# Attention and feed-forward in one kernel: constants built in three parts, two score pairs moved into the steps, products of ones, GEMM pieces and PSUM banks dealt out anew

## The chip, the cores and the metric

The kernel runs on one core of a Trainium2 chip. The metric is the time of one execution in device microseconds (us); lower is better. TensorE (PE, with its weight loads PEld), VectorE (DVE), ScalarE (ACT), GpSimd (POOL) and SyncE (SP, which here only issues DMAs) each run their own instructions in program order and wait for one another by semaphores.

## The reference, cut to what matters

```python
scores = scale * q @ k^T                                 # (4, 12, 448, 448): batch, head, row, column
scores = einsum('bhij,hg->bgij', scores, w_pre)          # premix: mixes the 12 heads
attn = exp(scores - max); attn = attn / (sum + 1e-9)
attn = einsum('bhij,hg->bgij', attn, w_post)             # postmix
x = (attn @ v), heads side by side                       # (1792, 768)
h = x @ w_in; r = maximum(h, 0); g = s * r * r + b       # w_in 768 x 2048
out = g @ w_out                                          # w_out 2048 x 768
```

All inputs are float32. The kernel keeps float32 accuracy by splitting an operand into a rounded high part and a low part, and adding three products (low by high, high by low, high by high).

## The kernel before, in words

**Chunks and blocks.** The rows of the scores are cut into 16 chunks (4 per batch, of 110 or 118 rows), and each chunk into 11 or 12 blocks of up to 10 rows, 180 blocks (`NB`) in all. A block holds 10 rows of all 12 heads on 120 partitions, so that the mixing of heads is a product with a 120x120 matrix (`wpre_hi`, `wpre_lo`: `w_pre` repeated along a diagonal of blocks; `wpost` likewise).

**Scores of a chunk.** `qk_part` (line 469) does a pair of heads in three products each; six pairs make a chunk. The result goes from PSUM into the tile `S` of the chunk with the scale 1/8. In most pairs both heads lie in the one two-bank PSUM tile `sc`, and one ACT instruction copies both (line 495). In chunks 0 and 1 the odd pairs are `apart`: each head takes a bank of its own, by `bank()`, and DVE copies them, one after the other (line 493). `relayout` (line 547) is a DMA on SP that gathers a block from all 12 heads of `S` into `blk`; it needs the whole chunk. `split` (line 555) on POOL makes the high and low part `hl` (lines 559, 560).

**Steps.** After a prologue the kernel runs one step `s` per block (line 805). In program order step `s` holds `relayout(s+5)`, `split(s+2)`, `normalize(s-1)` (DVE reciprocal, line 591; ACT scaling into `eh`, line 593), `evacuate(s-3)` (line 631 on DVE; line 629 on ACT for the last chunk), `premix(s)` (line 565: three products into a PSUM tile `pm`, DVE maximum on line 574, ACT exponential on line 579 in place, its sum on line 583), `remainder(s-1)` (DVE, line 600), `postmix(s-2)` (12 products on line 615), and what a plan puts there: loads of q, k, v, the transposes `prep_q` and `prep_k`, score pairs (`qk_pair`) of later chunks, pairs of attention times v (`av_pair`, line 513), pieces of the first GEMM (`head_piece`: three products on line 247). The plan is a list made at build time from costs and due times (lines 642 to 731). From step 12 on, each step also does one instruction of the conversion of a weight (`conversion`, lines 145 to 180).

**Prologue** (lines 756 to 803). Loads; then the pairs of chunk 0, among them the transposes of k by `prep_k`, whose low part is a DVE instruction (line 232) that is put off until the next `low_parts()`. `keep_busy(n)` issues n products of a tile of ones, 128x512, into a PSUM tile that nobody reads. Then `build_consts` (line 340): 14 DVE instructions that make `wpre_hi`, `wpre_lo`, the scale `xscale` and `wpost`. Then five relayouts, two splits, `prep_q` of chunk 1, and the six pairs of chunk 1.

**Tail of the attention and start of the GEMMs.** The first GEMM (`gemm1_part`, line 242) makes `ph` tiles of 18 products for batch b and a block f of 128 columns of `w_in`. Three of them (b = 0, f = 0 to 2) are done in 18 pieces ahead: 12 by the plan in steps 167 to 179, 6 after the last step. After the steps come conversions (`convert_to`), the last chunk's six `av_pair`s and the 6 pieces, one more conversion (line 842), the splitting of batch 1's x (`split_x`, lines 212 to 225: ACT line 223 for the high part, DVE line 232 for the low part), and the loop over the `ph` tiles; ACT's `relu2` (lines 252 to 267) takes each. Their banks come from `bank()` (line 237), which deals out six banks in the fixed order of `banks` = pm, po, pm, po, xp, px by a count `turn["bank"]`; the prologue's 22 calls have moved that count on. The pieces' tiles are `sc` (two banks) and, for f = 2, `px`. Two GEMM rounds follow, the second GEMM on line 300.

Of the kernel before, what the change touches and what calls it, by code (L numbers as in the profile page):

```python
# [21 lines left out]
def talking_heads_attention__then__act_relu2_kernel(  # L22
# [316 lines left out]

    def build_consts(mask, rep, wall):  # L340
        kron = smp.tile([BP, BI, H], F32, tag="kron", name="kron", bufs=1)
# [9 lines left out]

        mx = smp.tile([P, 4], F32, tag="mx", name="mx", bufs=1)
        nc.vector.tensor_reduce(out=mx[:, 0:1], in_=wall, axis=AX.X, op=ALU.max)
# [5 lines left out]
        nc.vector.tensor_scalar(mu[:, 3:4], mu[:, 2:3], 0x7F800000, None, op0=ALU.bitwise_xor)  # L359
        nc.vector.tensor_scalar_mul(xscale, mx[:, 2:3], 2.0 ** -29)  # L360
        kron2 = smp.tile([BP, H, BI], F32, tag="kron2", name="kron2", bufs=1)
        nc.vector.tensor_tensor(
# [106 lines left out]
    def qk_part(ci, p, m):  # L469
# [4 lines left out]
        qt, kt = q_t[ci], k_t[b, p]  # L474
        apart = ci < 2 and p % 2 == 1
        if m == 0 and apart:
# [14 lines left out]
        if apart:  # L491
            for e in range(2):
                nc.vector.tensor_scalar_mul(s_t[ci][:n, 2 * p + e, :], sc[e][:n, :S], SCALE)
        else:
            nc.scalar.activation(  # L495
                s_t[ci][:n, 2 * p:2 * p + 2, :], x_t["two"][:n, :, :S], AF.Copy, scale=SCALE
            )
# [67 lines left out]
    def premix(t):  # L565
        n = blocks[t][2] * H
        hl = hl_t.pop(t)

        tag = "px" if t % 3 == 2 else "pm"
        pm = ps.tile([P, 512], F32, tag=tag, name=f"pm_{t}", bufs=banks.count(tag))  # L570
        for m, (w, x) in enumerate(((wpre_lo, 0), (wpre_hi, 1), (wpre_hi, 0))):
            nc.tensor.matmul(pm[:n, :S], w[:n, :n], hl[:n, x, :], start=(m == 0), stop=(m == 2))  # L572
        st = smp.tile([BP, 4], F32, tag="st", name=f"st_{t}")
        nc.vector.tensor_reduce(  # L574
            out=st[:n, 0:1], in_=pm[:n, :S], axis=AX.X, op=ALU.max, negate=True
        )

        e = pm[:, :S]
        nc.scalar.activation(e[:n], e[:n], AF.Exp, bias=st[:n, 0:1], accum_out=pm[:n, S:S + 1])  # L579
        e_t[t] = (e, st)  # L580

        total = pm[:, S:S + 1]
        nc.scalar.activation(
            st[:n, 2:3], total[:n], AF.Copy, scale=2.0 ** -15, bias=1e-9 * 2.0 ** -15
        )
# [113 lines left out]
    for i in range(NHEAD * NKC):  # L699
        if i < NHEAD * NKC - LATE:  # L700
            when = w0 + i * (NB + 3 - w0) / (NHEAD * NKC - LATE)
            fill.append((when, w0 + i // 2, NB + 2, 0.567, 1, head_piece, ()))
        else:
# [71 lines left out]
    for p in range(NP):  # L775
        low_parts()
        if p + 2 < NP:
            prep_k(0, p + 2)
        if p == 1:
            low_parts()  # L780
            prep_q(0, 1)
            low_parts()
        for m in range(3):
            qk_part(0, p, m)
        if p < 3:
            keep_busy(1)
    banks.append("px")
    build_consts(*loaded_consts)
    for t in range(LD):
        relayout(t)  # L790
    for t in range(LS):
        split(t)

    for half in range(2):
        prep_q(1, half)
    low_parts()
    for p in range(NP):
        for m in range(3):
            qk_part(1, p, m)
    while plan[0][0] < 0:  # L800
        x = plan.pop(0)
# [3 lines left out]
    for s in range(NB + 3):  # L805
# [17 lines left out]
        if s < NB:  # L823
            premix(s)
        low_parts()
        if 0 <= s - 1 < NB:
            remainder(s - 1)
# [13 lines left out]
    run_plan(NB + 100, False)  # L841
    convert_to(NU_EARLY + 3)
    att.close()
# [6 lines left out]
    for kc in range(NKC):  # L850
        split_x(0, 1, kc)
        low_parts()
    for r in range(NR):
        u0 = 2 * r * NU
# [90 lines left out]
```

## Time and profile before

| | |
|---|---|
| time, median of 3 runs | 968.75 us (968.42 to 970.42) |
| the profiled execution: its own time | 969.14 us |
| its span, first to last instruction | 967.4 us |
| mean granted TensorE clock | 0.993 |
| busy: PE, DVE, ACT, POOL | 928.9, 640.2, 595.8, 397.1 us |
| steps 0 to 179 | premixes from 30.1 to 486 us of the span |
| first GEMM's first full tile, after the pieces | 500.95 us |

All times in the text are us from the start of the span. An engine that is idle costs time only where the work that ends last waits for it. A row of the timeline that holds several instructions of one line is marked x and their number; its duration is that of the lot.

### The profile page before, as it was taken

How to read it: one execution, taken by the hardware profiler on the slowest of the kernel's cores; microseconds unless marked ns; L12 is line 12 of the kernel's file. 1: busy time of each engine (PE TensorE's matmuls, PEld its weight loads, DVE VectorE, ACT ScalarE, POOL GpSimd, SP SyncE). 2: the span in 40 equal slices, each digit the busy share in tenths (PEclk: the TensorE clock that was granted, in tenths of full speed). 3: DMA queues.
4: the chain of work that ended last, by engine and by line, in shares of the span. 5: the costliest groups of instructions: out<-in, count | busy, mean ns of one | idle time of the engine just before them, and what ended most of it. 6: DMA issues, size and time to landing. Idle time of an engine off the chain costs nothing.

```text
span 967.4 us, 19864 instructions
## 1 busy us (share of the span) xinstructions
PE 928.9 (96%) x7515; PEld 786.4 (81%) x7515; DVE 640.2 (66%) x1314; ACT 595.8 (62%) x1315; POOL 397.1 (41%) x469
## 2 busy tenths in 40 slices
PE   6889999999999999999989999999999999999998
PEld 3656767777777777777779999999998999999998
DVE  4789999888878888788678217746716811849311
ACT  3587777777888888888777878422216787711000
POOL 3766667666676667666613323100001332310000
PEclk8899999999999999999999999999999999999999
DMA  4665645654455544645422302234431410237431
GB/s 103 165 152 143 173 115 147 174 135 136 122 138 145 134 129 116 154 123 160 121 70 90 123 23 84 82 115 139 147 139 42 154 59 1 69 112 215 144 99 50
DMA packets 124252, 114.63 MB, mean 118 GB/s; under 512 B 61656, under 2 KB 120044, under 8 KB 124156
## 3 DMA queue, kind: packets, MB, share of 16 engines
q1 hardware_dynamic: 114630, 101.69, 38.1%
q10 hardware_dynamic: 9366, 11.59, 3.4%
q8 instruction: 59, 0.97, 0.4%
q0 software_dynamic: 160, 0.09, 0.1%
q14 instruction: 37, 0.30, 0.1%
HBM read 58.28 MB, written 16.52 MB: 77 GB/s over the span
## 4 chain that ended last, share of the span: by engine, by line
PE 65%; ACT 14%; DVE 14%; DMA 4%; issue 2%; POOL 1%; SPq 0%; ACTq 0%; DVEq 0%; POOLq 0%
PE po L300 24%; PE ph L247 16%; PE po L615 6%; PE pm L572 5%; PE xp L513 5%; PE sc L485 5%; ACT S L495 4%; ACT pm L579 3%; DVE eh L600 3%; ACT eh L593 3%; DVE A L631 2%; DVE st L574 2%; DMA nq<-in_q_dram 1%; PE trk L438 1%; DMA blk<-S 1%
## 5 line engine op out<-in xcount | busy, mean ns | idle before, releaser
L300 PE MATMUL po<-w,g 128*128 128x384 f32 x1344 | 234.6, 336 | 2.6 <-ACT h L255 2.6
L300 PEld LDWEIGHTS po<-w,g 128*128 128x128 f32 x1344 | 233.7, 188 | 3.3 <-ACT h L255 3.2
L560 POOL TENSOR_TENSOR hl<-blk,hl 120x448 fp32r<-120x448 f32 x180 | 205.8, 1143 | 15.0
L265 POOL TENSOR_TENSOR g<-h,g 128x448 fp32r<-128x448 f32 x64 | 77.7, 1214 | 291.5 <-ACT g L264 278.2
L615 PEld LDWEIGHTS <-eh 120*128 120x128 f16 (+1 forms) x2160 | 115.8, 98 | 65.8 <-DVE eh L600 42.5
L247 PE MATMUL ph<-x,w 128*128 128x448 f32 x810 | 166.1, 364 | 0.0
L559 POOL TENSOR_SCALAR hl<-blk 120x448 fp32r<-120x448 f32 x180 | 104.5, 581 | 141.7 <-PE pm L572 124.5
L247 PEld LDWEIGHTS ph<-x,w 128*128 128x128 f32 x810 | 151.9, 188 | 12.1
L615 PE MATMUL po<-wpost,eh 120*128 120x120 f16 (+1 forms) x2160 | 145.6, 218 | 16.6 <-DVE eh L600 14.9
L579 ACT ACTIVATE pm<-pm,st 120x448 f32<-120x448 f32 x180 | 109.8, 610 | 56.4 <-DVE st L574 55.8
L600 DVE SCALAR_TENSOR_TENSOR eh<-pm,st,eh 120x448 f16<-120x448 f32 x180 | 122.1, 678 | 18.0 <-ACT eh L593 14.7
L593 ACT ACTIVATE eh<-pm,st 120x448 f16<-120x448 f32 x180 | 114.2, 634 | 18.5 <-DVE st L591 16.1
L574 DVE TENSOR_REDUCE st<-pm 120x1 f32<-120x448 f32 x180 | 111.0, 617 | 22.0 <-PE pm L572 20.5
L631 DVE COPY A<-po 128x480 f32<-128x480 f32 x168 | 106.8, 636 | 0.1
L572 PE MATMUL pm<-hl,wpre_hi 120*120 120x448 f32 x360 | 102.9, 367 | 0.7 <-POOL hl L560 0.7
L495 ACT ACTIVATE S<-sc 110x896 f32<-110x896 f32 (+1 forms) x90 | 82.5, 917 | 22.0 <-PE sc L485 17.5
L513 PE MATMUL xp<-A,v 128*64 128x110 f32 (+1 forms) x1536 | 93.7, 265 | 0.6 <-ACT A L629 0.6
L153 ACT ACTIVATE mk<-raw 128x384 f32<-128x384 f32 x64 | 35.4, 553 | 91.7 <-DMA raw<-in_moe_w_out_dram 35.0
L485 PE MATMUL sc<-Tk,Tq 64*110 64x448 f32 (+1 forms) x576 | 84.4, 400 | 5.6 <-DVE Tq L232 3.6
L513 PEld LDWEIGHTS xp<-A,v 128*64 128x64 f32 x1536 | 74.2, 136 | 10.2 <-ACT A L629 1.1
L572 PE MATMUL pm<-hl,wpre_lo 120*120 120x448 f32 x180 | 82.1, 456 | 0.0
L232 DVE TENSOR_TENSOR x<-xraw,x 128x448 fp32r<-128x448 f32 x36 | 24.1, 695 | 76.9 <-ACT x L223 76.9
(74 smaller groups left out, 999.8 us busy)
## 6 DMA issues: line engine op xcount, KB each, us to landing
blk<-S SPq DMA_DIRECT2D x172, 210.0 KB
raw<-in_moe_w_in_dram SPq DMA_DIRECT2D x32, 384.0 KB
raw<-in_moe_w_out_dram SPq DMA_DIRECT2D x32, 384.0 KB
xraw<-xd SPq DMA_DIRECT2D x48, 224.0 KB
part<-ob ACTq DMA_DIRECT2D x28, 192.0 KB
acc<-part SPq DMA_DIRECT2D x28, 192.0 KB
out_dram<-acc ACTq DMA_DIRECT2D x28, 192.0 KB
v<-in_v_dram SPq DMA_DIRECT2D x24, 192.0 KB
```

What stands on the lines that cost most here:

```text
L247: nc.tensor.matmul(ph[:, :S], w[:, i, c0:c0 + P], x[:, y, :], start=(kc == 0 and m == 0), stop=(kc == NKC - 1 and m == 2),)
L300: nc.tensor.matmul(po[:, :NO], g[:, x, c0:c0 + P], w[:, y, :], start=(f == 0 and m == 0), stop=(f == NF - 1 and m == 2),)
L485: nc.tensor.matmul(sc[e][:n, :S], qt[r0:r0 + D, p, x, :n], kt[r0:r0 + D, y, :], start=(m == 0), stop=(m == 2),)
L513: nc.tensor.matmul(xp[e * D:(e + 1) * D, p % 4, :n], vt[:, e, c, :], a[:, c, 2 * p + e, :n], start=(c == 0), stop=(c == NC - 1),)
L560: nc.gpsimd.tensor_tensor(out=hl[:n, 1, :], in0=blk[:n], in1=hl[:n, 0, :].bitcast(F32), op=ALU.subtract)
L572: nc.tensor.matmul(pm[:n, :S], w[:n, :n], hl[:n, x, :], start=(m == 0), stop=(m == 2))
L574: nc.vector.tensor_reduce(out=st[:n, 0:1], in_=pm[:n, :S], axis=AX.X, op=ALU.max, negate=True)
L579: nc.scalar.activation(e[:n], e[:n], AF.Exp, bias=st[:n, 0:1], accum_out=pm[:n, S:S + 1])
L593: nc.scalar.activation(eh[:n, 0, :], e[:n], AF.Copy, scale=st[:n, 3:4])
L600: nc.vector.scalar_tensor_tensor(out=eh[:n, 1, :], in0=e[:n], scalar=st[:n, 3:4], in1=eh[:n, 0, :], op0=ALU.mult, op1=ALU.subtract,)
L615: nc.tensor.matmul(po[:, c * BP:(c + 1) * BP], eh[:n, x, j0:j0 + P], wpost[:n, y].rearrange("p g i -> p (g i)"), start=(m == 0), stop=(m = ...
L631: nc.vector.tensor_copy(dst, src)
```

## The change

`build_consts` becomes three functions: `build_pre` (3 DVE instructions: the premix matrix) runs after `prep_q` of chunk 1 and ahead of its pairs, `build_scale` (7) within step 0, `build_post` (4) within step 1, each behind that step's premix. Chunk 1's pairs 4 and 5 move from the prologue into steps 0 and 1, right behind these; pair 5 now uses the two-bank tile. The copies of the remaining odd pairs are shared: ACT copies the first head, DVE the second. In the prologue the low part of k's last transpose is put ahead of pair 3, and one product of ones is dropped. `premix` gets products of ones into its own `pm` tile, ahead of its three: two in steps 0 to 9, one in steps 10 to 13, 24 in all. Of the 12 pieces that the plan spread, 8 are now spread over steps 167 to 175, and 4 kept for steps 179, 180 (two) and 181; two pairs of attention times v move with them. The count of the banks is set to 0 ahead of the GEMMs, and the conversion of line 842 is put behind `split_x` of batch 1.

```diff
--- before.py
+++ after.py
@@ -337,7 +337,9 @@
         nc.gpsimd.dma_start(sb[:, 1:2], moe_b.rearrange("(o n) -> o n", o=1).to_broadcast([P, 1]))
         return mask, rep, wall

-    def build_consts(mask, rep, wall):
+    mx = cst.tile([P, 4], F32, name="mx")
+
+    def build_pre(mask, rep, wall):
         kron = smp.tile([BP, BI, H], F32, tag="kron", name="kron", bufs=1)
         nc.vector.tensor_tensor(
             out=kron,
@@ -349,7 +351,7 @@
         nc.vector.tensor_copy(wpre_hi, kf)
         nc.vector.tensor_tensor(out=wpre_lo, in0=kf, in1=wpre_hi.bitcast(F32), op=ALU.subtract)

-        mx = smp.tile([P, 4], F32, tag="mx", name="mx", bufs=1)
+    def build_scale(mask, rep, wall):
         nc.vector.tensor_reduce(out=mx[:, 0:1], in_=wall, axis=AX.X, op=ALU.max)
         nc.vector.tensor_reduce(out=mx[:, 1:2], in_=wall, axis=AX.X, op=ALU.min, negate=True)
         nc.vector.tensor_tensor(out=mx[:, 0:1], in0=mx[:, 0:1], in1=mx[:, 1:2], op=ALU.max)
@@ -358,6 +360,8 @@
         nc.vector.tensor_scalar(mu[:, 2:3], mu[:, 0:1], 0x7F800000, None, op0=ALU.bitwise_and)
         nc.vector.tensor_scalar(mu[:, 3:4], mu[:, 2:3], 0x7F800000, None, op0=ALU.bitwise_xor)
         nc.vector.tensor_scalar_mul(xscale, mx[:, 2:3], 2.0 ** -29)
+
+    def build_post(mask, rep, wall):
         kron2 = smp.tile([BP, H, BI], F32, tag="kron2", name="kron2", bufs=1)
         nc.vector.tensor_tensor(
             out=kron2,
@@ -472,7 +476,7 @@
         if p == 0 and m == 0:
             s_t[ci] = sp.tile([CH, H, S], F32, tag="S", name=f"S_{ci}")
         qt, kt = q_t[ci], k_t[b, p]
-        apart = ci < 2 and p % 2 == 1
+        apart = ci < 2 and p % 2 == 1 and (ci, p) != (1, NP - 1)
         if m == 0 and apart:
             x_t["sc"] = [bank(f"sc_{ci}_{p}_{e}") for e in range(2)]
         elif m == 0:
@@ -489,8 +493,8 @@
         if m < 2:
             return
         if apart:
-            for e in range(2):
-                nc.vector.tensor_scalar_mul(s_t[ci][:n, 2 * p + e, :], sc[e][:n, :S], SCALE)
+            nc.scalar.activation(s_t[ci][:n, 2 * p, :], sc[0][:n, :S], AF.Copy, scale=SCALE)
+            nc.vector.tensor_scalar_mul(s_t[ci][:n, 2 * p + 1, :], sc[1][:n, :S], SCALE)
         else:
             nc.scalar.activation(
                 s_t[ci][:n, 2 * p:2 * p + 2, :], x_t["two"][:n, :, :S], AF.Copy, scale=SCALE
@@ -568,6 +572,8 @@

         tag = "px" if t % 3 == 2 else "pm"
         pm = ps.tile([P, 512], F32, tag=tag, name=f"pm_{t}", bufs=banks.count(tag))
+        for _ in range(2 if t < first[1] - 1 else 1 if t < first[1] + 3 else 0):
+            nc.tensor.matmul(pm, keep[:, :P], keep, start=True, stop=True)
         for m, (w, x) in enumerate(((wpre_lo, 0), (wpre_hi, 1), (wpre_hi, 0))):
             nc.tensor.matmul(pm[:n, :S], w[:n, :n], hl[:n, x, :], start=(m == 0), stop=(m == 2))
         st = smp.tile([BP, 4], F32, tag="st", name=f"st_{t}")
@@ -698,8 +704,12 @@
     w0 = first[NCH - 1] - XA + 2
     for i in range(NHEAD * NKC):
         if i < NHEAD * NKC - LATE:
-            when = w0 + i * (NB + 3 - w0) / (NHEAD * NKC - LATE)
-            fill.append((when, w0 + i // 2, NB + 2, 0.567, 1, head_piece, ()))
+            j = i - (NHEAD * NKC - LATE - 4)
+            if j < 0:
+                when = w0 + i * (NB - 1 - w0) / (NHEAD * NKC - LATE - 4)
+                fill.append((when, w0 + i // 2, NB + 2, 0.567, 1, head_piece, ()))
+            else:
+                at(NB - 1 + (0, 1, 1, 2)[j], 1, head_piece)
         else:
             fill.append((NB + 100, NB + 3, NB + 100, 0.567, 1, head_piece, ()))
     fill.sort(key=lambda x: x[0])
@@ -776,27 +786,27 @@
         low_parts()
         if p + 2 < NP:
             prep_k(0, p + 2)
+        if p in (1, 3):
+            low_parts()
         if p == 1:
-            low_parts()
             prep_q(0, 1)
             low_parts()
         for m in range(3):
             qk_part(0, p, m)
-        if p < 3:
+        if p < 2:
             keep_busy(1)
     banks.append("px")
-    build_consts(*loaded_consts)
     for t in range(LD):
         relayout(t)
-    for t in range(LS):
-        split(t)
-
     for half in range(2):
         prep_q(1, half)
     low_parts()
-    for p in range(NP):
+    build_pre(*loaded_consts)
+    for p in range(NP - 2):
         for m in range(3):
             qk_part(1, p, m)
+    for t in range(LS):
+        split(t)
     while plan[0][0] < 0:
         x = plan.pop(0)
         x[3](*x[4])
@@ -823,6 +833,9 @@
         if s < NB:
             premix(s)
         low_parts()
+        if s < 2:
+            (build_scale, build_post)[s](*loaded_consts)
+            qk_pair(1, NP - 2 + s)
         if 0 <= s - 1 < NB:
             remainder(s - 1)
         run_plan(s, True)
@@ -839,7 +852,7 @@
     convert_to(NU_EARLY + 2)
     run_plan(NB + 100, True)
     run_plan(NB + 100, False)
-    convert_to(NU_EARLY + 3)
+    turn["bank"] = 0
     att.close()

     mp = ctx.enter_context(tc.tile_pool(name="mp", bufs=2, reuse_waits="tile"))
@@ -850,6 +863,7 @@
     for kc in range(NKC):
         split_x(0, 1, kc)
         low_parts()
+    convert_to(NU_EARLY + 3)
     for r in range(NR):
         u0 = 2 * r * NU
         n = NHEAD if r == 0 else NF // 2
```

## Rows read from the trace of the kernel before

**Rows 1.** Windows: stretch, length, busy of each engine, granted clock, DMA share, GB/s.

```profile
65.00:70.00 5.00, 5.00 (x69) 3.85 (x66) 4.94 (x12) 3.96 (x10) 3.41 (x4) 1.00 0.56 147
...
470.00:480.00 10.00, 10.00 (x117) 8.01 (x115) 5.78 (x13) 8.64 (x23) 7.25 (x9) 1.00 0.48 150
...
30.00:34.00 4.00, 2.79 (x11) 1.39 (x9) 2.69 (x6) 2.33 (x6) 2.79 (x5) 1.00 0.65 161
34.00:38.00 4.00, 3.58 (x29) 3.10 (x30) 3.58 (x8) 3.02 (x10) 3.69 (x6) 0.61 0.61 152
```

**Rows 2.** Timeline, 16 to 32 us: start, duration, instruction [idle before <-releaser].

```profile
16.65 1.15 DVE L493 TENSOR_SCALAR S<-sc 110x448 f32<-110x448 f32 x2 [0.95 <-PE sc L485]
...
17.72 0.61 DVE L232 TENSOR_TENSOR Tk<-trk,Tk 128x448 fp32r<-128x448 f32 x1
...
18.39 0.87 PE L485 MATMUL sc<-Tk,Tq 64*110 64x448 f32 x6 [1.18 <-DVE Tk L232]
...
19.29 1.16 DVE L493 TENSOR_SCALAR S<-sc 110x448 f32<-110x448 f32 x2 [0.96 <-PE sc L485]
...
20.36 0.27 DVE L342 TENSOR_TENSOR kron<-mask,rep 120x120 f32<-120x120 f32 x1
...
20.53 6.44 SPq L552 DMA_DIRECT2D blk<-S  x5
...
23.25 0.28 DVE L372 TENSOR_TENSOR wpost<-kron,wpost 120x120 f16<-120x120 f32 x1
...
24.11 4.39 PE L485 MATMUL sc<-Tk,Tq 64*110 64x448 f32 x22 [3.24 <-DVE Tq L232]
24.84 0.56 POOL L559 TENSOR_SCALAR hl<-blk 120x448 fp32r<-120x448 f32 x1 [9.87 <-DMA blk<-S]
...
25.48 1.14 POOL L560 TENSOR_TENSOR hl<-blk,hl 120x448 fp32r<-120x448 f32 x1
...
30.38 0.57 PE L572 MATMUL pm<-hl,wpre_hi 120*120 120x448 f32 x2
...
31.26 0.61 DVE L574 TENSOR_REDUCE st<-pm 120x1 f32<-120x448 f32 x1
```

**Rows 3.** Timeline: maximum of steps 4 and 13; copy of a pair.

```profile
39.66 0.61 DVE L574 TENSOR_REDUCE st<-pm 120x1 f32<-120x448 f32 x1
...
48.22 0.92 ACT L495 ACTIVATE S<-sc 110x896 f32<-110x896 f32 x1 [0.46 <-DMA v<-in_v_dram]
...
61.01 0.60 DVE L574 TENSOR_REDUCE st<-pm 120x1 f32<-120x448 f32 x1
```

**Rows 4.** Timeline, SP's queue and POOL, steps 8 to 13.

```profile
50.49 1.30 SPq L552 DMA_DIRECT2D blk<-S  x1
...
56.51 0.57 POOL L559 TENSOR_SCALAR hl<-blk 120x448 fp32r<-120x448 f32 x1 [0.49 <-DMA blk<-S]
```

**Rows 5.** Timeline (first two) and line 591's instructions: DVE beside POOL.

```profile
589.42 0.35 DVE L175 TENSOR_SCALAR u<-w 128x384 uint32<-128x384 uint32 x1
...
601.96 1.31 DVE L175 TENSOR_SCALAR u<-w 128x384 uint32<-128x384 uint32 x1
...
L591 DVE RECIPROCAL st<-st x180: 144/163/166, 32.8 to 488.0; 120x1 f32<-120x1 f32 x172, 108x1 f32<-108x1 f32 x8
```

**Rows 6.** Timeline, from the last steps to the first GEMM.

```profile
489.71 0.80 PE L615 MATMUL po<-wpost,eh 108*128 108x120 f16 x12 [1.15 <-DVE eh L600]
...
491.13 5.06 PE L513 MATMUL xp<-A,v 128*64 128x118 f32 x96 [0.62 <-ACT A L629]
...
497.05 0.36 DVE L154 TENSOR_SCALAR u<-raw 128x384 uint32<-128x384 uint32 x1
...
500.19 3.29 DVE L232 TENSOR_TENSOR xg<-xraw,xg 128x448 fp32r<-128x448 f32 x6
...
500.95 3.95 PE L247 MATMUL ph<-xg,w 128*128 128x448 f32 x18 [0.95 <-DVE xg L232]
...
505.80 7.70 PE L247 MATMUL ph<-xg,w 128*128 128x448 f32 x36 [0.91 <-ACT h L255]
```

## The prediction

> **What bounds the kernel now.** I read busy time by windows first, then the timeline of every stretch that the diff touches, with the chain of waits beside it. PE is the engine that is full: from 65 us on, in the last steps before 480 us [rows 1], and in the GEMMs. So what can be gained is idle time of PE, or time in which PE works slowly. Three places are not full, and the change touches just these.
>
> *Prologue.* DVE is the bound. It copies both heads of an odd pair in turn (1.15 us), and behind that stands the low part of k's last transpose, for which pair 5 waits 1.18 us; then come pair 5's own two copies, which end chunk 0's scores at 20.45 [rows 2]. Two things hang on that end: SP's first relayout at 20.53 and the 14 instructions for the constants, from 20.36 to 23.53, behind which stand the low parts of q that chunk 1's pairs wait 3.24 us for. The first block lands for POOL at 24.84, but PE is busy with chunk 1 until 30, so the first premix ends at about 30.95 (30.38 + 0.57) and the first maximum of a step starts at 31.26 [rows 2].
>
> *Steps 0 to 13.* Here PE waits for a loop of DVE and ACT (reciprocal, maximum, exponential, sum). From the maximum of step 4 to that of step 13 it takes 21.35 us, 2.37 us a step [rows 3]. SP's queue issues 28 DMAs end to start from the first relayout at 20.53 [rows 2] to block 13's at 50.49, which lands late: POOL waits for it until 56.51 [rows 4].
>
> *The turn to the GEMMs.* PE waits 1.15 us for the last remainder, 0.62 us for the last evacuation, 0.95 us for x's low parts, and 0.91 us for a bank that ACT still reads [rows 6].
>
> **The change, part by part.** *Copies on two engines, low part first.* The low part can now start before pair 3's copy, at 16.65 at the latest, and ends 0.61 us later; pair 5 then starts when PE is done with pair 4, at about 17.25 (its start of 18.39 less the 1.18 it waited). It takes 0.87, and the two copies lie beside each other: DVE's half is 1.16/2 = 0.58, ACT's between 0.46 and 0.92 (half of a pair's copy, or all of it [rows 3]); I take 0.6. Chunk 0's scores end at about 18.75 instead of 20.45, **1.7 us earlier**, and so does SP's whole queue. Bounds: 1.2 to 1.9.
>
> *Constants in parts, two pairs moved.* Only 3 of the 14 instructions stay ahead of chunk 1, so its four pairs are done well before block 0 lands, at 24.84 - 1.7 = 23.1; what hides them is that wait for the DMA. POOL's split takes from 24.84 to 26.62, 1.78 us, and premix's last two products 0.57: step 0's maximum starts at about 25.5 instead of 31.26, **5.8 us earlier**. What was moved now lies in steps 0 and 1. On DVE 11 of the 14 instructions, by their count 2.5 of the 3.17 us; on ACT two copies of 0.92 us each, beside them; on PE twice 0.87, in its idle time. Queued behind them on DVE are the reciprocal and remainder of step 0, behind the copies on ACT the scaling of step 0. DVE's 2.5 us is the longer sum, so step 4's maximum is 5.8 - 2.5 = 3.3 us earlier if steps 0 to 4 else take their 8.40 us (31.26 to 39.66). Part of that time was half clock (0.61 from 34 to 38 [rows 1]), and in steps 0 and 1 the old order had DVE copying pair 5; without both up to 1.2 us more could come. So 3.3 to 4.5, and I take 4.1: the clock was down for most of steps 3 and 4.
>
> *What DVE pays beside POOL.* In the prologue POOL was idle while DVE built the constants. In steps 0 and 1 POOL splits one block after another. A DVE instruction on SBUF that takes 0.35 us alone took 1.31 beside a POOL instruction; the reciprocal on 120x1 elements never took over 0.166 in 180 [rows 5]. Of the 11 instructions 5 are of one element a partition, like it, and 2 are reductions of 144; 4 are 120 wide. I charge nothing for the 5, and for the other 6 between 0 and 0.96 each; as the waits end together with POOL's instruction, I take about a quarter, **1.5 us in all** (0 to 5.8). By the Trainium skill, page "SBUF — State Buffer", section "SBUF: two separate sides", DVE and POOL hold a shared port pair as an exclusive lock for a whole instruction, and the other one blocks fully. By that page of the Trainium skill the four wide ones would wait each for one POOL instruction, about 3 us instead of 1.5, and the sum would be 3.45 instead of 4.95; the two rows on line 175 agree with the lock, the reciprocal shows that it does not touch all.
>
> So the steps' own chain brings 4.1 - 1.5 = **2.6 us**. *What is late next* is block 13: SP's queue is 1.7 us earlier, so POOL can start it at 54.8, step 13's maximum comes at 54.8 + 1.78 + 0.57 = 57.2, against 61.01: 3.8 us is the most that can be kept. Later steps are full on PE and move as a whole.
>
> *Products of ones.* By the GEMM's rows a product of 448 columns takes 0.214 us at the full clock (7.70/36 [rows 6]), so one of 512 about 0.24, two in a step 0.49. They stand ahead of a premix, on PE, where a step of 2.37 us leaves idle time (PE 2.79 of 4.00 at 30 to 34 us); 24 cost nothing while that lasts. If they hold the clock up, they save part of the 1.2 named above. The product dropped in the prologue lies ahead of a PE wait: nothing.
>
> *Head pieces.* Three pieces of 3 x 0.214 = 0.64 us leave the full stretch and go to where PE waited 1.15 and 0.62. If every step were as long as PE's work that would be 1.8 us. But the pairs of attention times v are dealt out anew with them: by the plan's own arithmetic steps 175 and 177 get no pair now, and a step with little PE work falls back on the loop of DVE and ACT. I take **0.5 us** (0 to 1.8).
>
> *Banks and x first.* With the count at 0 the first two full tiles take a `pm` and a `po` bank, which the last steps have left; before, the second one took `px`, in which piece tile 2 stood. With the conversion behind `split_x`, x's low parts start one conversion earlier (3.14 us, from 497.05 to 500.19 [rows 6]), and each is there before PE needs it. Both waits go, 0.95 + 0.91: **1.85 us** (1.0 to 1.9). The conversion put back is late next; its weight is for a tile five places on, at 3.85 us each (7.70/2).
>
> **The sum.** 2.6 + 0.5 + 1.85 = 4.95 us. The profiled execution took 969.14 us around a span of 967.4; the median is 968.75, 0.4 below. On the median's scale: **963.8 us**.
>
> **Rivals.** *SP's queue decides.* If the stage ends by DMA alone, it gains the 1.7 us of SP's start: 1.7 + 0.5 + 1.85 = 4.05, 964.7 us. For it: no pause in SP's queue. Against: at step 13 the loop was 2.2 us behind block 13 (61.01 less 56.51 less 1.78 and 0.57). It lies in the forecast's range: 0.15.
>
> *The loop decides, without the port.* The constants cost DVE no more than before, the clock stays up, and the gain is held only by block 13: 3.8 + 0.5 to 0.9 + 1.85, 962.4 us. For it: the reciprocal's row. 0.18.
>
> *The lock in full.* Each of the 6 larger instructions waits 0.96: 4.1 - 5.8 spends the prologue's gain and 1.7 us more at step 4, which the later waits for blocks take up in part; POOL itself would stand still soon for want of premixes, which ends it. I put the first stage at 0.3 us and the sum at 2.6: 966.1 us. For it: line 175. [...] 0.15.
>
> *Slower: the clock.* If PE has the half clock in the new steps 0 to 9, its work of about 1.65 us a step (2.79 of 4.00 busy, 2.37 us a step) becomes 3.3, with the products of ones 4.3, 1.9 us over the pace. The whole gain of 4.95 is gone after three such steps, some 13 us, and with ten it would be 983 us. For it: at 34 us the clock fell while PE was busy for 2.79 of 4.00 us before. Against: it came back within 4 us, and the products add to just that activity. 0.04.
>
> *It doesn't do what it says:* if the pieces and banks bring nothing because other waits stand in the same places, 2.6 to 3.4 remain, 965.8 us: 0.08.
>
> **How the numbers follow.** The forecast has 0.40, the rivals 0.15, 0.18, 0.15, 0.04 and 0.08. The range from 961.3 (3.8 + 1.8 + 1.9) to 967.2 (0 for the first stage, 1.5 for the turn) leaves out the slower rival and parts of the lock and of the last one. A measurement of this kernel can tell about 0.2%, 1.9 us, from no change: faster means below 966.8. All but the slower rival and a part of the lock and of the last rival lie below: 0.87 faster, 0.09 within, 0.04 slower.
>
> **What would show it.** First relayout on SP at about 18.8; step 0's maximum at about 25.5; DVE's L362 to L372 longer than 0.28 if the port counts; step 13's maximum at 57.2 to 59; no wait of PE for remainder, evacuation, x or ACT's h between the last steps and the first full tiles. Wrong would be: a first relayout after 20, a PE clock of half in the new steps 0 to 5, a maximum of step 13 later than 60.5, or a new wait of PE behind the first full tiles.

## The result, and the profile after

The changed kernel took 959.39 us (median of 4 runs, 958.7 to 961.09) beside 969.37 for the kernel before on the same chip (968.42 to 970.42): ratio 0.9906, 95% interval 0.989 to 0.9922. That is faster by 7.6 to 10.7 us, as forecast in sign, but by about twice the 4.95 of the sum, and outside the range of 961.3 to 967.2 on the fast side. The profiled execution took 961.09 around a span of 959.4, 8.0 less than the 967.4 of before; it was the slowest of its four, and a later trace of the same kernel has 958.4.

In what follows a ratio is the median time over that of the kernel before, run beside it on the same chip, with its 95% interval in brackets. "Step 13" with a time is the start of that step's maximum, and a lead is how much earlier something starts than in the first trace of the kernel before.

The timeline of the prologue and of steps 0 and 1 after, cut to the rows that answer to [rows 2] (start, duration, engine, line; in brackets the idle time ahead and what ended it):

```profile
18.85 6.20 SPq L556 DMA_DIRECT2D blk<-S  x5
...
23.08 0.56 POOL L563 TENSOR_SCALAR hl<-blk 120x448 fp32r<-120x448 f32 x1 [8.19 <-DMA blk<-S]
...
25.47 1.14 POOL L564 TENSOR_TENSOR hl<-blk,hl 120x448 fp32r<-120x448 f32 x1
...
25.61 0.62 DVE L580 TENSOR_REDUCE st<-pm 120x1 f32<-120x448 f32 x1 [1.89 <-PE pm L578]
26.15 0.29 DVE L355 TENSOR_REDUCE mx<-wall 128x1 f32<-128x144 f32 x1
...
26.68 0.47 DVE L357 TENSOR_TENSOR mx<-mx 128x1 f32<-128x1 f32 x1
...
27.38 0.15 DVE L360 TENSOR_SCALAR mx<-mx 128x1 uint32<-128x1 uint32 x1
...
28.59 0.52 DVE L372 TENSOR_SCALAR kron<-kron,mx 120x120 f32<-120x120 f32 x1
...
29.12 1.14 POOL L564 TENSOR_TENSOR hl<-blk,hl 120x448 fp32r<-120x448 f32 x1
...
29.15 1.19 DVE L375 CAST wpost<-kron 120x120 f16<-120x120 f32 x1
...
30.37 0.54 DVE L376 TENSOR_TENSOR wpost<-kron,wpost 120x120 f16<-120x120 f32 x1
30.84 0.67 DVE L606 SCALAR_TENSOR_TENSOR eh<-pm,st,eh 120x448 f16<-120x448 f32 x1
```

SP's first relayout starts at 18.85 and step 0's maximum (L580) at 25.61; 18.8 and 25.5 were forecast. Step 0's remainder (L606) waits behind the moved constants until 30.84. TensorE's clock differs too: in the kernel before it was granted at half until 4.1, from 7.6 to 11.0, 21.2 to 28.0 and 34.9 to 38.3, in the changed kernel until 9.9, and from there it was full until 958.8. Step 13's maximum is 3.33 earlier than before (61.01):

```profile
57.68 0.60 DVE L580 TENSOR_REDUCE st<-pm 120x1 f32<-120x448 f32 x1
```

PE at the turn to the GEMMs, to be held against [rows 6]:

```profile
482.33 0.80 PE L621 MATMUL po<-wpost,eh 108*128 108x120 f16 x12 [0.31 <-DVE eh L606]
482.95 1.46 PE L247 MATMUL ph_head<-x,w 128*128 128x448 f32 x6
...
485.92 5.06 PE L517 MATMUL xp<-A,v 128*64 128x118 f32 x96
490.91 3.88 PE L247 MATMUL ph_head<-x,w 128*128 128x448 f32 x18
494.62 11.11 PE L247 MATMUL ph<-xg,w 128*128 128x448 f32 x54
```

Of the four waits of before (1.15, 0.62, 0.95, 0.91) 0.31 is left; the pieces fill their place, and three full tiles follow without a gap. Put together, the lead over the kernel before, from the starts in both traces: 5.66 at step 0, 3.27 at step 4, 3.33 at step 13 (forecast 2.6), 3.45 at step 61, **4.33 at step 68**, 4.77 at step 166 (forecast still 2.6), 5.21 at the last chunk's products of A and v (491.13 less 485.92), 6.33 at the first full tile, 7.53 at the second, 7.78 at the fourth, 8.0 at the end. Two more traces of the kernel before, taken later, qualify the first of these: their step 13 is at 59.6 and 59.7, so that the lead over them is 1.93 and 2.04 there, 3.86 and 4.26 at step 166, and 7.1 and 7.4 at the end.

### The profile page after: what moved, and what is told of

Same layout as the page of the kernel before. It is cut to its first block, busy times and chain, and to the rows that moved or that the text cites. A ratio compares the mean times of both kernels' runs of the same rounds, so it can differ in the third digit from the quotient of the medians.

```text
span 959.4 us, 19910 instructions
## 1 busy us (share of the span) xinstructions
PE 929.8 (97%) x7538; PEld 786.2 (82%) x7538; DVE 639.0 (67%) x1307; ACT 597.7 (62%) x1321; POOL 398.1 (41%) x469
## 3 DMA queue, kind: packets, MB, share of 16 engines
q1 hardware_dynamic: 114630, 101.69, 38.3%
## 4 chain that ended last, share of the span: by engine, by line
PE 64%; ACT 15%; DVE 13%; DMA 5%; issue 2%; POOL 0%; SPq 0%; ACTq 0%; DVEq 0%
PE po L300 24%; PE ph L247 17%; PE xp L517 6%; PE po L621 5%; ACT S L499 5%; PE sc L489 5%; PE pm L578 5%; ACT pm L585 4%; ACT eh L599 3%; DVE eh L606 3%; DVE A L637 2%; DVE st L580 2%; DMA raw<-in_moe_w_out_dram 2%; DMA nq<-in_q_dram 1%; PE trk L442 1%
## 5 line engine op out<-in xcount | busy, mean ns | idle before, releaser
L564 POOL TENSOR_TENSOR hl<-blk,hl 120x448 fp32r<-120x448 f32 x180 | 206.0, 1145 | 15.0
L606 DVE SCALAR_TENSOR_TENSOR eh<-pm,st,eh 120x448 f16<-120x448 f32 x180 | 122.1, 679 | 16.6 <-ACT eh L599 13.2
L580 DVE TENSOR_REDUCE st<-pm 120x1 f32<-120x448 f32 x180 | 110.9, 616 | 22.0 <-PE pm L578 20.4
L153 ACT ACTIVATE mk<-raw 128x384 f32<-128x384 f32 x64 | 35.5, 554 | 93.7 <-DMA raw<-in_moe_w_out_dram 43.9
```

The source lines that it names most:

```text
L564: nc.gpsimd.tensor_tensor(out=hl[:n, 1, :], in0=blk[:n], in1=hl[:n, 0, :].bitcast(F32), op=ALU.subtract)
L580: nc.vector.tensor_reduce(out=st[:n, 0:1], in_=pm[:n, :S], axis=AX.X, op=ALU.max, negate=True)
L606: nc.vector.scalar_tensor_tensor(out=eh[:n, 1, :], in0=e[:n], scalar=st[:n, 3:4], in1=eh[:n, 0, :], op0=ALU.mult, op1=ALU.subtract,)
```

## The experiments

Theory: the gain is what the sum names, with terms mis-sized, plus a wait in mid run that got shorter. Rivals: that the part in mid run is chance, that the end's gain hangs on the front's, that the products of ones carry the front. Where only part of the change stands, the rest is as before.

**Front alone** (copies, low part, constants in three, pairs in steps), from the changed kernel:

```diff
-        for _ in range(2 if t < first[1] - 1 else 1 if t < first[1] + 3 else 0):
-            nc.tensor.matmul(pm, keep[:, :P], keep, start=True, stop=True)
...
-    turn["bank"] = 0
```

with head pieces, conversion and the dropped product of the prologue as before too.

> Left in: only the front of the change (copies on two engines, low part first, constants in three, two pairs within steps 0 and 1). Left as before: no products of ones, head pieces, banks and conversion. Theory 1 (the waits in mid run, steps 55 to 100, shrink because the whole queue of DMAs started earlier): step 13's maximum 3.3 us earlier than before as in the changed kernel, 4.7 by step 100, and the time 4.7 us under the kernel before (ratio 0.995). Theory 2 (mid run is chance from execution to execution): 3.3 earlier at step 13 and between 2.5 and 5 at step 100, ratio 0.996 or 0.997. Theory 3 (the products of ones carry part of the front): the clock falls to half around 20 to 38 us as before, step 4's maximum gains at most 2.5 instead of 3.27.

962.66 us, ratio 0.994 (0.9928 to 0.9953). Step 13 leads by 3.96 and step 100 by 5.32: the part in mid run came again (as in theory 1; what makes it is taken up below). The clock was at full from 5.3 (9.9 in the changed kernel), hence the larger lead, and at half from 29.2 to 36.0; step 4 still led by 3.84, so theory 3 fails as put. At the turn, PE:

```profile
485.81 6.72 PE L517 MATMUL xp<-A,v 128*64 128x118 f32 x96 [0.62 <-ACT A L633]
492.46 3.88 PE L247 MATMUL ph_head<-x,w 128*128 128x448 f32 x18
496.41 11.21 PE L247 MATMUL ph<-xg,w 128*128 128x448 f32 x54
```

The 96 products took 6.72 at half clock (486.6 to 490.0) instead of 5.06, and behind these 1.66 the wait of 0.95 for x's low parts doesn't show. The wait of 0.91 for a bank is gone too, without the reset: pair 5 of chunk 1 no longer calls `bank()` twice, the count is 20 instead of 22, and the first two tiles take `pm` and `po` anyway.

**End alone** (heads, banks, conversion), from the kernel before:

```diff
-    convert_to(NU_EARLY + 3)
+    turn["bank"] = 0
     att.close()
...
         low_parts()
+    convert_to(NU_EARLY + 3)
     for r in range(NR):
```

and the plan's hunk of the change.

> The kernel before with the three edits at the end alone: four head pieces kept, banks begun anew, conversion behind split_x. If the parts add up: step 13's and step 100's maxima as before within 0.3 us, chunk 4's last products of A and v 0.45 us earlier, the full tiles 3.0 us earlier, 965.7 to 966.4 beside 969.0 (ratio 0.997). The rival, that the end's gain hangs on the earlier front: under 1.5 us (ratio 0.9985 or above).

965.61 us, ratio 0.9968 (0.9957 to 0.998), with hardly a lead at step 166 (0.09) and 2.89 at the third full tile. So the end has its gain without the front, and that rival is out. The percentages add up, 0.6 and 0.32 beside 0.94 together, but not term by term: the bank's wait is gone in both kernels, and the profiled execution of the front alone paid 1.66 of half clock at the turn.

**Without the products of ones:** the two lines of the diff of the front alone taken out, nothing else.

> The changed kernel without the 24 products of ones. My prediction's theory (they cost nothing and may save part of 1.2 us of half clock): 0 to 1.2 us slower than the changed kernel, with the granted clock at half somewhere between 21 and 38 us. The rival (they only take PE's time): as fast or up to 1 us faster, clock at full throughout. A stronger form of the first: the clock falls as long as before (about 10 us in all) and step 13's maximum is 1.5 us or more later.

960.6 us, ratio 0.9917 (0.9904 to 0.993). The windows of this kernel and then of the changed one (PE, PEld, DVE, ACT, POOL busy, then the granted clock):

```profile
28.00:32.00 4.00, 2.09 (x14) 1.34 (x15) 3.90 (x8) 2.46 (x7) 3.83 (x7) 0.82 0.63 156
32.00:36.00 4.00, 4.00 (x30) 3.52 (x28) 2.94 (x8) 2.46 (x8) 1.79 (x4) 0.50 0.62 157
```

```profile
28.00:32.00 4.00, 2.43 (x20) 1.54 (x20) 3.90 (x8) 2.46 (x7) 3.83 (x7) 1.00 0.66 166
32.00:36.00 4.00, 4.00 (x47) 3.19 (x44) 3.39 (x9) 3.25 (x10) 2.24 (x5) 1.00 0.62 153
```

Without them the clock is at half from 30.5 to 37.4, and step 13 comes 0.94 later (58.62). The first reading holds in the trace; in the time the intervals of the two kernels overlap. The fall doesn't come in every execution: of the five runs the fastest, 959.0, had a mean granted clock of 1.0, the other four 0.996.

**The changed kernel again**, unchanged.

> The changed kernel unchanged, for a second trace. If the shorter waits in mid run belong to the kernel: step 13's maximum at 57.7 within 0.2 us, step 100's 1.4 us further ahead of the kernel before than step 13's. If they are chance: the gain at step 100 differs by 0.7 us or more from the first trace's 4.75. The time is 958.7 to 961.1 as before.

960.11 us, ratio 0.9909 (0.9896 to 0.9923). Step 13 at 57.81, step 68 ahead by 4.21, step 100 by 4.62: the part in mid run belongs to the kernel. This span is 1.0 shorter almost wholly by one wait, PE's for the last `h` ahead of the second GEMM's last round, here and in the first trace:

```profile
840.33 4.95 PE L300 MATMUL po<-w,g 128*128 128x384 f32 x27 [0.28 <-ACT h L255]
```

```profile
841.31 3.94 PE L300 MATMUL po<-w,g 128*128 128x384 f32 x21 [1.24 <-ACT h L255]
```

**Constants whole in the prologue**, the rest changed:

```diff
     build_pre(*loaded_consts)
+    build_scale(*loaded_consts)
+    build_post(*loaded_consts)
...
-            (build_scale, build_post)[s](*loaded_consts)
```

> The changed kernel with all three parts of the constants in the prologue, ahead of chunk 1, where its first part stands. Theory 1 (DVE waits beside POOL for the moved constants, 1.5 us as I charged, 1.8 by the rows of after): L356 to L375 take their short durations again, step 0's maximum is at most 0.5 later than 25.6 (hidden behind block 0), step 4's 1.5 to 2 earlier, of which step 13 keeps up to 1 (block 13's limit), and the time is 0.5 to 1.5 us under the changed kernel. Rival (the place costs nothing, DVE's sum is the same anywhere): chunk 1's low parts wait 2.3 us, step 0's maximum comes 1 to 2 us later, and step 13 and the time stay or grow by up to 1 us.

958.79 us, ratio 0.9902 (0.9884 to 0.992). DVE's rows for the same instructions:

```profile
21.40 0.16 DVE L357 TENSOR_TENSOR mx<-mx 128x1 f32<-128x1 f32 x1
...
22.41 0.28 DVE L372 TENSOR_SCALAR kron<-kron,mx 120x120 f32<-120x120 f32 x1
22.73 0.22 DVE L375 CAST wpost<-kron 120x120 f16<-120x120 f32 x1
22.99 0.28 DVE L376 TENSOR_TENSOR wpost<-kron,wpost 120x120 f16<-120x120 f32 x1
...
28.67 0.68 DVE L606 SCALAR_TENSOR_TENSOR eh<-pm,st,eh 120x448 f16<-120x448 f32 x1 [0.40 <-ACT eh L599]
```

Theory 1: the four take 0.94 together instead of 2.72 beside POOL, step 0's maximum moves by 0.09 only, step 4's comes 1.25 and step 13's 1.67 earlier. But of the 1.67 only 0.61 is left at step 54 and 0.42 at the full tiles. In the change, then, the place of the constants gives back 1.8 us on DVE and, by the trace, about half a microsecond at the turn; in the time the intervals of the two kernels overlap, so there it is not shown.

**Banks alone**, **conversion alone** and **head pieces alone**, each of the three edits of the end by itself in the kernel before.

> The kernel before with the banks begun anew and nothing else. My prediction's term: the wait of 0.91 for ACT ahead of the second full tile goes, the one for x's low parts ahead of the first (0.95) stays, time about 0.9 under before (ratio 0.999). If the bank also held back the first tile: up to 1.9.

> The kernel before with the conversion put behind split_x and nothing else. My prediction's term: the wait of 0.95 for x's low parts goes, the one of 0.91 for the bank stays, time about 0.95 under before (ratio 0.999). If the first full tile is paced by x's low parts all the way through, as its trace after the change suggests: 1.3 to 1.8 (the rest of the 2.57 measured at the turn).

> The kernel before with the four head pieces kept for the last steps, nothing else. My prediction's term was 0.5 (0 to 1.8). If the parts of the end add up: the last products of A and v start 0.45 earlier, the waits for x (0.95) and for ACT's bank (0.91) stay, time 0.4 to 0.5 under the kernel before (ratio 0.9995). If they take each other's place: x's low parts, which do not come earlier, make PE wait 0.45 longer ahead of the first full tile, and the time is the same.

Banks: 966.82 us, ratio 0.9987 (0.9973 to 1.0001), an interval that just takes in no change. PE's rows after the pieces show the first wait left, the second gone; the second tile starts 3.81 behind the first instead of 4.85, 1.04 less:

```profile
503.09 9.14 PE L247 MATMUL ph<-xg,w 128*128 128x448 f32 x43 [0.85 <-DVE xg L232]
```

Conversion: **slower**, 971.6 us, ratio 1.0029 (1.0016 to 1.0043):

```profile
491.21 6.72 PE L513 MATMUL xp<-A,v 128*64 128x118 f32 x96 [0.62 <-ACT A L629]
497.87 3.87 PE L247 MATMUL ph_head<-x,w 128*128 128x448 f32 x18
501.58 3.88 PE L247 MATMUL ph<-xg,w 128*128 128x448 f32 x18
507.38 4.87 PE L247 MATMUL ph<-xg,w 128*128 128x448 f32 x15 [1.92 <-ACT h L255]
```

The wait for x is gone, but the wait for ACT's bank has grown from 0.91 to 1.92: the second tile takes up all that the first gained. The clock was at half twice (491.5 to 494.9, 508.5 to 512.0), 1.66 by the 96 products alone. The lower clock goes with the edit: seven of its ten runs had a mean granted clock of 0.991 or 0.992, and one of the 23 runs of the kernel before beside them. How the edit would bring the clock down is not shown; the trace of the front alone had the first of the two falls as well, without it. The other three runs of the conversion alone took 969.5 to 969.91, no less than the 968.08 of the kernel before, so that it gained nothing in them either.

Head pieces: 967.46 us, ratio 0.998 (0.9969 to 0.9992). The trace shows PE's wait for `eh` down from 1.15 to 0.33 and the last products of A and v starting 0.43 earlier, counted from step 166, and the waits for x (0.98) and ACT (0.97) standing. By the interval the time fell by at least 0.8 us; what the rest of it is, the trace doesn't say.

**Copies and low part alone**, in the kernel before (run twice), and **the copies undone** in the changed kernel:

```diff
-            for e in range(2):
-                nc.vector.tensor_scalar_mul(s_t[ci][:n, 2 * p + e, :], sc[e][:n, :S], SCALE)
+            nc.scalar.activation(s_t[ci][:n, 2 * p, :], sc[0][:n, :S], AF.Copy, scale=SCALE)
+            nc.vector.tensor_scalar_mul(s_t[ci][:n, 2 * p + 1, :], sc[1][:n, :S], SCALE)
...
+        if p in (1, 3):
+            low_parts()
         if p == 1:
-            low_parts()
```

> The kernel before with the copies of odd pairs on two engines and the low part put first, nothing else. My prediction's first term: chunk 0's scores end 1.7 earlier and SP's first relayout comes at about 18.8 instead of 20.53; chunk 1 still stands behind the whole of the constants, so step 0's maximum is 1.7 to 2.5 earlier. Mid run: if the relayouts that land at 195.4 to 195.5 in the kernels with the old front are held by SP's queue from its start on, they land 1.7 earlier or so; if the stretch in mid run has a pace of its own, they land at 195.4 whatever the front, and the front's gain is lost there down to at most 1.0.

> The changed kernel with both copies of an odd pair on DVE again, one behind the other; the low part stays first. Theory: SP's first relayout at 19.5 to 20 instead of 18.85, step 13's maximum 0.3 to 0.8 later than the changed kernel's 57.7, the time 0.3 to 0.8 above it. Rival (the loop of the steps hides it): step 13 within 0.2 and the time the same. Mid run: if the shorter wait there hangs on SP's start, it grows by about the same 0.6 to 1.1; if on the steps' earlier start, it stays under 0.4.

Alone: 964.9 us, ratio 0.9969 (0.9956 to 0.9982), first relayout at 19.07, where kernels with the old front and a clock that rose as late, at 10 to 11, have 20.65 to 20.89: the forecast 1.7. Undone: 961.48 us, ratio 0.9925 (0.9907 to 0.9943), first relayout at 19.51, step 13 at 58.22, 0.54 later; no longer wait in mid run. Of these 0.66 the clock has 0.14, since it rose 0.4 later and the low part already started at 16.67 instead of 16.53. So about 0.5 of the 1.7 is the copies' and about 1.2 the low part's.

**Products of ones alone**, and **one more of them in the prologue** of the changed kernel (`if p < 3` for `p < 2`):

> The kernel before with the 24 products of ones and nothing else. My prediction's reasons: they cost nothing and save up to 1.2 of half clock in steps 0 to 9. Theory: the fall at 34 to 38 does not come, step 13's maximum 0.5 to 1.2 earlier, the time up to 1.2 under the kernel before. Rival: the clock is decided by the idle stretch at 20 to 24 us, falls as before, and the products, at half speed, cost 0.2 to 1.5. Mid run: the relayouts land at 195.4 as in the other kernels with the old front, so that a gain of the steps is lost again there and the wait of 1.24 grows by it.

> The changed kernel with one more product of ones in the prologue, behind pair 2 as before the change. Theory 1 (what PE did there sets when the clock rises, 5.3 us in the front alone and 9.9 in the changed kernel): full clock from about 5.3, first relayout at 17.4 instead of 18.85, step 0's maximum at 24.1, step 13's 0.3 to 0.7 earlier, time 0.3 to 0.7 under the changed kernel. Rival (the time of the first rise differs from execution to execution whatever the code): rise at about 10, first relayout 18.9 to 19.1, no difference.

Alone: 969.13 us, ratio 1.0002 (0.999 to 1.0014). The fall at 34 does not come, one at 19.0 to 25.8 does. Step 13 is at 59.85; two more traces of the kernel before, whose clock rose as early (below), have 59.6 and 59.7, so nothing is gained there. Later ACT waits 1.82 at step 65, and PE 2.64 for x at the turn: the conversion ahead of x's low parts waited for a weight to land, DVE 1.78 and ACT 1.90. One more in the prologue: 960.73 us, ratio 0.9925 (0.9908 to 0.9943), clock up at 10.8, first relayout 19.41. Theory 1 falls: the first rise is not set by that product. Nor do the traces look like the rival's chance from execution to execution: those of one kernel agree (9.9 and 10.0 in the changed kernel; 9.9 and 10.1 in the copies alone; 4.1, 4.4 and 4.6 in the kernel before). What sets it is not found.

**The wait in mid run.** The lead grows most between steps 61 and 68 (0.88), at one ACT copy of a score pair. The row of the kernel before, then of the changed one:

```profile
195.39 0.92 ACT L495 ACTIVATE S<-sc 118x896 f32<-118x896 f32 x1 [1.24 <-DMA blk<-S]
```

```profile
190.95 0.92 ACT L499 ACTIVATE S<-sc 118x896 f32<-118x896 f32 x1 [0.26 <-DMA blk<-S]
```

The copy writes into an `S` tile that a relayout still reads. To see whether this is chance, the kernel before ran twice more for a trace, and the copies alone once more:

> The kernel before, unchanged, for a second trace. If the wait at step 65 belongs to the kernel: again 1 to 1.5 us for the relayout ahead of the copy that started at 195.39, steps 64 to 65 3.1 to 3.4 apart. If it differs from execution to execution: under 0.5 or over 2, and the steps 2.5 apart where it is absent.

> The kernel before, unchanged, for a third trace. As for the second: a wait of 1 to 1.5 at step 65 if it belongs to the kernel; under 0.5 or over 2 if not.

> The kernel before with the copies on two engines and the low part first alone, for a second trace. If the wait at step 65 belongs to the kernel: absent again, steps 64 to 65 2.5 apart. If it differs from execution to execution, it may well stand here with 0.6 to 2.5. First relayout at 19.1 as in its first trace, or up to 1.5 earlier if the clock rises early.

968.16 and 968.52 us: waits of 1.63 and 1.97, so the kernel before had it in each of its three traces, of differing size. The copies alone, 966.76 us: steps 64 and 65 lie 3.89 apart, in the first trace 2.49 (no wait). SP's rows of the two executions of this one kernel, first and second:

```profile
171.23 0.72 SPq L380 DMA_DIRECT2D v<-in_v_dram  x1
172.00 0.85 SPq L383 DMA_DIRECT2D v<-in_v_dram  x1
172.95 1.68 SPq L552 DMA_DIRECT2D blk<-S  x2
```

```profile
169.85 2.18 SPq L380 DMA_DIRECT2D v<-in_v_dram  x1
172.08 0.67 SPq L383 DMA_DIRECT2D v<-in_v_dram  x1
172.85 1.69 SPq L552 DMA_DIRECT2D blk<-S  x2
```

The second one's queue was 1.4 ahead, and one load held it for 2.18 instead of 0.72; behind it the two are level. Last, **the two pairs put back** ahead of the steps in the changed kernel, and **moved alone** in the kernel before:

```diff
-    for p in range(NP - 2):
+    for p in range(NP):
...
-            qk_pair(1, NP - 2 + s)
```

> The changed kernel with all six pairs of chunk 1 ahead of the steps again (the constants stay in three parts). If the pairs are what the first stage gains: step 0's maximum 1.5 to 3 later than 25.6, step 13's 1 to 2 later than 57.7, time 1 to 2 above the changed kernel. If the constants are: step 0's maximum within 1 of 25.6, step 13's within 0.5, and the time the same or, since ACT's two copies no longer lie in steps 0 and 1, up to 0.5 less. If the wait at step 65 goes with the pairs: steps 64 to 65 3 to 4 us apart here; if not: 2.5.

> The kernel before with the last two pairs of chunk 1 moved into steps 0 and 1, nothing else. If the pairs are what the first stage gains: step 0's maximum 2 to 4 earlier than 31.26, step 13's 1 to 2 earlier than 61.0 (or 59.6 where the clock rises early), time 1 to 2 under the kernel before. If the constants are: step 13 within 0.5 of the other traces of the kernel before. If the wait at step 65 goes with the pairs: steps 64 to 65 2.5 apart here; if not: 3 to 4.

Put back: 964.03 us, ratio 0.9938 (0.9916 to 0.996), 3.1 us behind the changed kernel by the ratios and 3.4 by the spans. Block 0 was there at 21.55, but PE did pairs 4 and 5 first, so step 0's maximum came at 25.78; the clock was at half from 32.1 to 35.5, step 13 came 1.92 later than in the changed kernel (what the pairs and what the clock have of that, no run separates), and the wait is back:

```profile
194.28 0.92 ACT L499 ACTIVATE S<-sc 118x896 f32<-118x896 f32 x1 [1.63 <-DMA blk<-S]
```

Moved alone: 967.0 us, ratio 0.998 (0.9969 to 0.9991): step 0 1.62 earlier, step 13 0.73 earlier than in the first trace of the kernel before and 0.6 to 0.7 later than in the other two; the bank's wait is gone by the count (1.1); steps 64 and 65 lie 3.12 apart.

Over all traces with the steps: in the eight where step 61 starts before 185.2 (the changed kernel and those near it, all with the pairs in the steps) steps 64 and 65 lie 2.5 apart; of the twelve where it starts after 185.4, eleven have 2.76 to 4.59, and one has 2.49. So this gain goes with an early front. SP's queue tells more: from the store `xd<-xs` at 167 to 172 to the last of the four relayouts ahead of that copy it has the same 21 issues in every trace. They take 17.7 to 20.7 us in the nine traces without the wait, and the queue pauses between two of them for 0.35 to 1.55 at the longest; in the eleven with the wait they take 20.8 to 22.7, and it never pauses for more than 0.27. In the kernel before (21.3, longest pause 0.11) the queue itself is the bound in this stretch, in the changed kernel (20.1, 0.56) it is not. Why the same issues take longer in the later fronts is not found.

**A faster version still:** the constants whole in the prologue, and the conversion that stood ahead of the last `relu2` on ACT behind it:

```diff
-            if b == B - 1:
-                convert_to(done["conv"] + 1)
+            if b == B - 1 and i != len(order) - 2:
+                convert_to(done["conv"] + (2 if i == len(order) - 1 else 1))
```

> The changed kernel with the constants whole in the prologue, and at each end of the first GEMM the one conversion that stands ahead of the last tile's evacuation on ACT put behind it. Theory (that conversion is what PE waits for before the second GEMM, 1.2 us in round 1 and 0.3 to 1.6 in round 2): both waits fall by 0.5 or more, 0.5 to 1.5 under the kernel with the constants whole (958.8). Rival (the chain of the evacuation itself, 2.5 us on ACT and 1.2 to 1.5 on GpSimd, sets the wait): no difference, or later weights make PE wait elsewhere, up to 1 slower.

957.06 us (955.91 to 957.93), ratio 0.9882 (0.9864 to 0.99), the lowest of all; its interval overlaps that of the constants whole and, by its edge, that of the changed kernel. PE's wait ahead of the second GEMM's first round (1.20 in the changed kernel) is gone. In the last round 0.23 is left, but there the second trace of the changed kernel had 0.28 without the edit:

```profile
838.14 4.11 PE L300 MATMUL po<-w,g 128*128 128x384 f32 x22 [0.23 <-ACT h L255]
```

## Why the prediction was right, and where it was wrong

*Copies and low part, 1.7:* right, 1.6 to 1.7 between kernels whose clock rose at the same time: first relayouts at 20.65 (old front) and 19.07 (new) with the rise at 10.1 to 10.2, 20.82 and 19.18 with it at 10.7, 18.98 and 17.31 with it at 4.8. That 18.85 stands beside the 20.53 of the prediction's own trace is in part luck: that trace had a fall of the clock from 7.6 to 11.0, and the other two of the kernel before have 18.91 and 18.89, no later than the changed kernel.

*Step 0's maximum 5.8 earlier:* right, 5.66. *The moved work:* I let it cost 2.5 on DVE and 1.5 for the port, less 0.8, so that 2.6 were left at step 4. There 3.27 were left, 3.33 at step 13. The port was sized well in place: four instructions took 1.78 more than with POOL idle. I charged six, the two reductions among them, and these kept their 0.29; the 128x1 one that I charged nothing for as "of one element" took 0.47 instead of 0.16. The Trainium skill, page "SBUF — State Buffer", section "SBUF: two separate sides", names DVE's two-port modes and instructions with two SBUF inputs as those that take the lock, the latter only against a GpSimd instruction that reads SBUF. The trace agrees: L357 and L376 have two SBUF inputs and grew, the one-input reductions and L360 did not, nor did L366 (0.27), whose two SBUF inputs lay beside POOL's MEMSET, which reads none; L375 ended at 30.34, when POOL's L564 did (30.26). That condition, which I had left out, picks the right ones of those; whether L372 and L375 run in such a mode no row shows. What the port took in steps 0 and 1 was partly taken back by waits that come later anyway (1.67 at step 13, 0.42 at the full tiles). The two pairs, whose work I put at nothing beside DVE, count most: putting them back cost more than undoing any other single part that was tried in the changed kernel (3.4 us of the span, a fall of the clock included). They leave PE free for premix 0 and give it work in steps 0 and 1.

*Products of ones, 0 and part of 1.2:* right in the trace (0.94 at step 13), too small to show in the time, and no gain found without the rest of the front.

*Head pieces, 0.5:* right, 0.44.

*Banks and x first, 1.85:* the mechanism was right, the size was not. The two starts moved by 6.33 less 5.21 and 7.53 less 6.33, 1.12 and 1.20 where I had the idle rows of 0.95 and 0.91: an idle row counts less than the stream of products loses around it (the tile of 18 products ahead of the second wait takes 3.95 with its end, in the stream of after 3.65). With 0.25 more in the next two tiles it is 2.57. The two are not a sum of independent terms either: the conversion alone passes its 0.95 on to the bank's wait. And the reset I credited was not needed, since the moved pair had put the count right.

**The step that failed** is "Later steps are full on PE and move as a whole". PE is full there on average, but the lead grew from 3.33 to 4.77 between steps 13 and 166 (over the other two traces of the kernel before by 1.9 and 2.2): the kernel before waits at step 65 for a relayout, with SP's queue full, and the changed kernel does not. Of the 1.44 that wait has 0.88 (1.26 and 1.61 over the other two traces); the rest, 0.12 before it and 0.44 in small steps behind it, is not traced to a wait. I had looked for DMA waits only up to block 13. The sum, by trace: 2.6 should have been 3.3, 0 in mid run 1.4, 0.5 stands (0.44), 1.85 should have been 2.57, and 0.2 came in the second round: 8.0. Of these the 3.3 hangs on the trace it is held against: over the other two traces of the kernel before the steps' own chain brought 1.9 and 2.0, less than the 2.6. The growth in mid run, which the prediction put at nothing, and the turn (2.57, 2.37 and 2.42) exceed it in all three. What the ratio has beyond these sums is 1 to 2 us; the wait ahead of the last round, 0.28 or 1.24 in two executions of the changed kernel, is one place of it, the rest is not found.

*Rivals.* None was it. Nearest was the loop without the port (962.4), for the wrong reason: the port counted, and was paid from elsewhere. SP's queue did not decide at block 13, but it did at step 65. The slower clock did not come: it was full from 9.9 to 958.8.

## What to carry to other kernels

An average of 96% busy doesn't make a stretch rigid: list the longest waits for DMAs all through the run before you say that a lead is kept as it is, neither more nor less. Take a second trace of the kernel before ahead of the sum: two of three traces here put step 13 1.3 to 1.4 us earlier than the one that the prediction read. Price a removed wait by how far the next start moves, not by its idle row, and test removals together, because one alone can hand its time to the next wait. A round-robin count is shared state: moving a call that uses it moves everything behind.

## What was not expected of the hardware

The first rise to the full clock (products of ones, 128x512, start 0.43 us apart until then and 0.21 to 0.23 after it) lies at 4.1 to 5.4 us in some kernels and at 9.8 to 10.8 in others, even where the prologue is the same code (4.1, 4.4 and 4.6 in three traces of the kernel before, 10.7 with the end alone), and the first relayout moves with it (19.00 with the products of ones alone, up at 5.4; 20.82 with the pairs alone, up at 10.7), unless the clock falls back, as from 7.6 to 11.0 in the first trace of the kernel before (4.1, but 20.53). A 128x1 DVE instruction with two SBUF inputs can take 0.47 (changed kernel) or 0.78 (pairs put back) instead of 0.16 beside POOL, while one-element instructions with one input stay at 0.15. One DMA issue on SP took 0.72 or 2.18 us in two executions of one kernel, so that a queue 1.4 ahead was level again after it, and the same 21 issues took 17.7 to 22.7.
